# Constant matrices loaded from DRAM in place of being computed on chip, with all engine orders renewed, in a one-core SSM and gated long-convolution kernel

## The chip, the cores and the metric

The kernel runs on one core of a Trainium2 chip. The metric is device time in microseconds (us) of one execution. Five engines share the work: TensorE (PE, with its weight loads PEld), VectorE (DVE), ScalarE (ACT), GpSimd (POOL) and SyncE (SP), which here only issues DMAs.

## What is computed

Length L = 2048, 448 channels, state size N = 256. `A` is a diagonal complex SSM turned into a convolution kernel of length 2048 per channel; `B` is a gated convolution with a given kernel; a sigmoid gate mixes them.

```python
def A(u):                                  # S4 part
    K = Re sum_n C[d,n] * dt*B[d,n] * exp(dt*(A_re+1j*A_im)[d,n] * l)      # l = 0..2047 rounded to bf16
    return irfft(rfft(K, 4096) * rfft(u, 4096))[:2048] + u * Dskip
def B(q, k, v):                            # H3 part
    kv = (short convolution of k with 4 taps, shift_k) * v
    return q * (irfft(rfft(kv, 4096) * rfft(ssm_k, 4096))[:2048] + kv * ssm_D)
x = A_u;  g = sigmoid((x * gate_w).sum(-1, keepdims=True))
out = g * A(x) + (1 - g) * B(x, B_k, B_v)
```

## The kernel before, in words

The 448 channels are cut into four groups `H` of 112. A long convolution is done as a Fourier transform in stages of matmuls: `spread` (a matmul with the matrix `Wc` or `WcK`), `transform` (with `W2`, tile `s_W`), `products` on VectorE, and back with `stage_a` (matrix `R`) and `stage_b` (matrix `G`). Every stage ends in a copy out of PSUM, done by ScalarE or VectorE. `conv_B(H)` does this for part B, `conv_A(H, ..)` for part A, `table(H)` makes the SSM kernel of a group: exponentials on ScalarE (`exps`), phases and sines (`levels`), long products on VectorE (`tables`, tiles TQ and TP), a sum over states on TensorE (`sums`) and a selection of rows with one-hot matrices (`gather`). `mix` joins the halves.

Ahead of that stands a setup. `Modes.run` transposes A, B and C on TensorE with an identity, and VectorE multiplies them by dt into the tile `hold`; the four transposing DMAs of k fill `kT` (tile natu and one slot q); VectorE makes the diagonal matrices `dg` out of the taps `shift_k`; TensorE then does the short convolution of k with them (matmuls `q,natu` and `q,q`); the copies of its result are multiplied by v into natv. When the last matmul of this has read `kT`, the same tile natu takes u (`natu<-in_A_u`).

All constants are made on chip. `Consts` makes index columns with GpSimd's iota and VectorE's bit operations; `stage_c`, `stage_a` and the phases of `stage_2` and `stage_b` are turned into sines by ScalarE, `stage_2` and `stage_b` after 16 matmuls of digits with rates; `rows` and `gather` make the one-hot matrices `sel` out of 29 iotas; identity, minus identity, `one`, `sel_d` and `gx` are made by comparisons.

Nothing is left to a scheduler on the engines: `Order` collects all calls, and the string `ORDER` lists in which order they are issued, which sets the order on each engine and each queue. `SLOTS` and `ROOMS` say which of the seven SBUF slots (q0 to q6) and four PSUM rooms (ps0 to ps3) each piece takes, `SIDES` whether VectorE (V) or ScalarE (S) does a copy, a negation or a phase shift by a quarter turn (`ahead`, on ScalarE with the column `quarter`). All instructions carry the line of `issue`, L137 (L130 after the change), so tiles tell them apart, not lines. DMAs of SP and ACT use eight semaphores in turn (DMAHW0 to DMAHW7): a DMA waits until the one before it on its semaphore has landed.

Of the kernel before, what the change touches and what calls it, by code (L numbers as in the profile page):

```python
# [1014 lines left out]
```

## Time and profile before

| what | us |
|---|---|
| median of 3 runs (lowest to highest) | 261.32 (261.09 to 261.94) |
| span of the profiled execution, first to last instruction | 258.0 |
| median of the runs less that span | 3.3 |
| busy: DVE, ACT, PE, PEld, POOL | 233.3, 208.2, 205.7, 187.0, 31.0 |
| data moved by DMA | 26.44 MB, 102 GB/s on average |
| mean granted clock of TensorE | 0.963 |

The profile gives a span and no time of its own for that execution; the median of the runs stands 3.3 us above the span, and this is taken as what lies around it. Busy shares are averages over a setup (the first 50 us, in which TensorE has little to do), a long middle part in which three engines are busy nearly all the time, and an end in which the last convolution and the stores are left. The window rows below separate these.

### The profile page before, as it was taken

How to read it: one execution, taken by the hardware profiler on the slowest of the kernel's cores; microseconds unless marked ns; L12 is line 12 of the kernel's file. 1: busy time of each engine (PE TensorE's matmuls, PEld its weight loads, DVE VectorE, ACT ScalarE, POOL GpSimd, SP SyncE). 2: the span in 40 equal slices, each digit the busy share in tenths (PEclk: the TensorE clock that was granted, in tenths of full speed). 3: DMA queues.
4: the chain of work that ended last, by engine and by line, in shares of the span. 5: the costliest groups of instructions: out<-in, count | busy, mean ns of one | idle time of the engine just before them, and what ended most of it. 6: DMA issues, size and time to landing. Idle time of an engine off the chain costs nothing.

```text
span 258.0 us, 12418 instructions
## 1 busy us (share of the span) xinstructions
PE 205.7 (80%) x5631; PEld 187.0 (72%) x5631; DVE 233.3 (90%) x374; ACT 208.2 (81%) x290; POOL 31.0 (12%) x81
## 2 busy tenths in 40 slices
PE   0714679888589898989789899988999988899820
PEld 0601179887478797989778899977899967889820
DVE  6899999999788999999999999997999999958930
ACT  4829978999489999999999999999999975455300
POOL 8970002020000002100000111000121120000000
PEclk9999979999899999999999999999999999799985
DMA  6999991499872547155123327300362188000096
GB/s 147 216 195 171 171 199 24 90 176 189 148 145 37 127 127 146 35 113 131 24 64 86 74 51 167 74 5 18 78 128 39 40 176 186 5 5 3 3 176 112
DMA packets 58917, 26.44 MB, mean 102 GB/s; under 512 B 49520, under 2 KB 57200, under 8 KB 58864
## 3 DMA queue, kind: packets, MB, share of 16 engines
q1 hardware_dynamic: 52192, 18.65, 38.4%
q0 software_dynamic: 2160, 5.51, 11.9%
q10 hardware_dynamic: 4512, 1.49, 3.1%
q8 instruction: 44, 0.72, 1.2%
q14 instruction: 9, 0.07, 0.1%
HBM read 8.17 MB, written 2.52 MB: 41 GB/s over the span
## 4 chain that ended last, share of the span: by engine, by line
PE 34%; ACT 26%; DVE 17%; DMA 9%; issue 6%; SPq 3%; ACTq 0%; DVEq 0%
PE ps L137 34%; ACT q L137 22%; DVE q L137 6%; DMA natu<-in_A_u_dram 5%; DVE TP L137 5%; SPq L137 3%; DMA q<-in_A_A_re_dram 2%; DMA q<-q 2%; ACT ET L137 2%; DVE G L137 1%; ACT RK L137 1%; DVE ET L137 1%; DVE RK L137 1%; DVE natv L137 1%; ACT L137 1%
## 5 line engine op out<-in xcount | busy, mean ns | idle before, releaser
L137 ACT CAST q<-ps 128x896 bf16<-128x896 f32 (+4 forms) x165 | 137.9, 927 | 18.3 <-PE ps L137 17.0
L137 PEld LDWEIGHTS <-q 128*128 128x128 bf16 (+2 forms) x720 | 51.5, 147 | 14.1 <-issue 6.3
L137 DVE TENSOR_TENSOR TQ<-TQ,ET 128x896 bf16<-128x896 bf16 (+2 forms) x70 | 45.7, 689 | 0.1
L137 PE MATMUL ps<-q,s_W 128*128 128x112 bf16 (+1 forms) x544 | 32.8, 211 | 6.1 <-ACT q L137 5.4
L137 PE MATMUL ps<-TP,TQ 128*32 128x32 bf16 x1792 | 32.9, 240 | 3.5 <-issue 2.4
L137 PE MATMUL ps<-sa_R,q 128*128 128x128 bf16 x448 | 33.6, 229 | 1.8 <-ACT q L137 0.9
L137 PEld LDWEIGHTS <-TQ 128*32 128x32 bf16 x1792 | 30.0, 153 | 5.7 <-issue 3.5
L137 PEld LDWEIGHTS <-s_W 128*128 128x128 bf16 x544 | 27.4, 98 | 8.5 <-issue 6.8
L137 DVE TENSOR_TENSOR q<-q,q 128x3584 bf16<-128x3584 bf16 (+1 forms) x22 | 32.6, 1511 | 0.3 <-DMA q<-q 0.3
L137 POOL DMA_DIRECT2D TP<-TP x15 | 13.0, 891 | 158.7 <-DVE TP L137 41.6
L137 PEld LDWEIGHTS <-G 128*128 128x128 bf16 x1024 | 28.1, 96 | 5.1 <-issue 2.6
L137 DVE TENSOR_TENSOR TP<-TP,ET 128x1792 bf16<-128x1792 bf16 (+3 forms) x25 | 31.6, 1274 | 0.0
L137 PEld LDWEIGHTS <-natu 128*32 128x32 bf16 (+1 forms) x560 | 27.9, 181 | 4.8 <-issue 4.4
L137 PE MATMUL ps<-q,G 128*128 128x28 bf16 x1024 | 29.0, 175 | 3.0 <-issue 1.6
L137 ACT ACTIVATE q<-hold 128x224 bf16<-128x224 f32 x64 | 22.1, 407 | 0.8 <-DVE hold L137 0.8
L137 ACT ACTIVATE ET<-q 128x1344 bf16<-128x1344 int16 (+1 forms) x12 | 17.4, 1454 | 1.2 <-DVE q L137 1.1
L137 DVE TENSOR_SCALAR q<-hold 128x224 int32<-128x224 f32 x40 | 14.8, 421 | 2.8 <-ACT ET L137 2.7
L137 PE MATMUL ps<-q,q 128*32 128x336 bf16 (+3 forms) x112 | 15.0, 300 | 2.6 <-DVE q L137 2.6
L137 PE MATMUL ps<-TP 128*128 128x512 bf16 x16 | 7.8, 614 | 10.7 <-POOL TP L137 5.1
L137 PE MATMUL ps<-Wc,natv 128*64 128x128 bf16 x224 | 15.0, 284 | 1.3 <-DVE natv L137 0.9
L137 PE MATMUL ps<-q,natu 128*32 128x336 bf16 (+3 forms) x336 | 15.4, 301 | 0.5 <-DVE q L137 0.4
L137 DVE TENSOR_TENSOR TQ<-TQ 128x448 bf16<-128x448 bf16 (+2 forms) x35 | 15.6, 450 | 0.1
(82 smaller groups left out, 267.4 us busy)
## 6 DMA issues: line engine op xcount, KB each, us to landing
q<-q SPq DMA_DIRECT2D x64, 112.0 KB, 3.3
TP<-TP POOLq DMA_DIRECT2D x9, 448.0 KB, 5.1
natv<-in_B_v_dram SPq DMA_DIRECT2D x4, 448.0 KB, 7.0
...
natu<-in_A_u_dram SPq DMA_DIRECT2D x4, 448.0 KB, 10.7
...
```

Of the source, the lines that this page charges most:

```text
L137: ins = f(*args, **kw)
```

## The change

Five DRAM constants are written into the program (`inline_tensor`) and loaded by six DMAs on ACT's queue: a tile `small` takes identity and `Wc` in one DMA (128x384 bf16) and `R`, minus identity, `one`, `sel_d`, `WcK` and `sel` in another (128x1248 bf16); `W2` is one DMA (128x4096 bf16); `gx` with four mask columns is one (128x132 f32); the packed `G` is two (128x2048 bf16 each). Each half of `G` is still spread into four column groups on chip by a multiplication with a mask column (`scaled`), seven of the eight on VectorE and one on ScalarE by the new `SIDES`. All iotas, index columns, comparisons, sines and the 16 matmuls of the old constants are gone. The strings `SLOTS`, `ROOMS`, `SIDES` and `ORDER` are new from the first character to the last.

```diff
 SIDES = (
-    "SSSSSSSSSSSSSSSSSSSSSSSSSSSSSSSSSSSSSSSSSSSSSVSSSSSSSSSSSSSSSSSSVVVVVVVSS...
+    "VVSVVVVVSSSSSSSSSSSVSSSSSSSSSSSSSSSSSSSSSSSSSSSSSSSSSSSSSSSSSSSSSVSVSSSS...
 ORDER = (
-    "1 225 69 104 106 105 109 108 207 223 67-68 111 214 210-211 63 75 64 116 32 2 208 20 ...
+    "10 4 12 1 23 15 111 11 13-14 24 0 5 16 46 49-65 700 2138 706 703 709 2132 67 716 714 ...
+class Consts:
+    def __init__(self, tc, nc, pool):
+        ...
+        self.small = (
+            ("ident", 128, lambda p, c: float(p == c)),
+            ("Wc", 256, lambda p, c: turns((p % 32) * (4 * (c // 4 % 32) + 1), 128, 1 + c // 128) if c % 4 == p // 32 else 0.0),
+            ("R", 256, ...), ("minus", 128, ...), ("one", 32, ...), ("sel_d", 32, ...), ("WcK", 256, ...), ("sel", 32 * n, ...),
+        )
+        ...
+        self.tile = pool.tile([P, total], bf16, name="small")
+    def dram(self, name, cols, value, dtype=bf16):
+        return self.tc.nc.inline_tensor(np.array(table(P, cols, value), dtype=mybir.dt.np(dtype)), name="c_" + name).ap()
+    def load(self, queue, names):
+        ...
+        queue.dma_start(self.tile[:, a:b], self.dram(names[0], b - a, ...))
+    # class Sides
+    def scaled(self, dst, src, col):
+        if self.vector():
+            self.nc.vector.tensor_scalar(out=dst, in0=src, scalar1=col, scalar2=None, op0=ALU.mult)
+        else:
+            self.nc.scalar.activation(dst, src, ACT.Identity, scale=col)
     # body
-    cons = Consts(nc, wp, shaped(arena["TP"][:], [3584], i32), evac)
-    cons.rows()
+    cons = Consts(tc, nc, wp)
+    cons.load(nc.scalar, ["ident", "Wc"])
+    W2 = wp.tile([P, 32, 2, 64], bf16, name="s2_W")
+    nc.scalar.dma_start(W2[:].rearrange("p k r s -> p (k r s)"), w2)
+    cons.load(nc.scalar, ["R", "minus", "one", "sel_d", "WcK", "sel"])
+    gx = wp.tile([P, 196], f32, name="gx")
+    nc.scalar.dma_start(gx[:, 64:196], cons.dram("gx", 132, ..., f32))
+    packed = shaped(arena["TP"][:], [2, 32, 2, 32], at=10240)
+    for i in range(2):
+        nc.scalar.dma_start(packed[:, i].rearrange("p b r a -> p (b r a)"), gd[:, 2048 * i:2048 * i + 2048])
+        for g in range(4):
+            evac.scaled(G[:, 32 * i:32 * i + 32, :, g, :].rearrange("p b r a -> p (b r) a"), packed[:, i]..., gx[:, 192 + g:193 + g])
-    Wc = cons.stage_c("Wc", a1, maskg)
-    cons.turns()
-    W2 = cons.stage_2(places)
-    R = cons.stage_a(...)
-    cons.stage_b(places, G, cons.onehot(4, cons.field(0, 3)), room)
-    cons.gather(q_half, maskg)
-    WcK = cons.stage_c("WcK", aK, cons.onehot(4, cons.field(3, 3)))
```

VectorE's first rows change as follows. Before, the work on constants (TP, Wc, WcK) stands between the setup's own rows (`hold`, and the phases `q<-hold`):

```order
L137 TENSOR_TENSOR WcK<-TP 128x256
L137 TENSOR_TENSOR hold<-ps_84,TP 128x8x2x28
L137 TENSOR_SCALAR TP<-TP 128x64
L137 TENSOR_SCALAR TP<-TP 128x4
L137 TENSOR_TENSOR Wc<-TP 128x256
L137 TENSOR_SCALAR TP<-TP 128x64 x2
L137 TENSOR_SCALAR TP<-TP 128x1
L137 TENSOR_TENSOR TP<-TP 128x1
L137 TENSOR_TENSOR hold<-ps_84,TP 128x8x2x28
L137 TENSOR_SCALAR q_80<-hold 128x224
L137 TENSOR_SCALAR q_81<-hold 128x224 x2
```

Of the change, on VectorE from its first row on (`gx` holds the mask columns, RK the column dt):

```order
L906 UNCONDITIONAL_BRANCH
L130 TENSOR_SCALAR G<-TP,gx 128x64x32 x4
L130 TENSOR_TENSOR hold<-ps_84,RK 128x8x2x28 x2
L130 TENSOR_SCALAR q_80<-hold 128x224
L130 TENSOR_SCALAR q_81<-hold 128x224
L130 TENSOR_SCALAR q_80<-hold 128x224
L130 TENSOR_TENSOR q_83<-ps_84,RK 128x8x2x28
L130 TENSOR_SCALAR q_80<-hold 128x224
```

The constants' rows are gone, and half of the spreading of `G` has moved to VectorE's very start, where it waits for two loads (`G`'s first half and `gx`).

On SP's queue the loads before stand so (modes A, B, C, then the transposing DMAs of k, with gate weights between them):

```order
L137 DMA q_77<-in_A_B_re_dram 112x4x256
L137 DMA q_79<-in_A_C_re_dram 112x4x256
L137 DMA q_79<-in_A_C_im_dram 112x4x256
L137 DMA_TRANSPOSE natu<-in_B_k_dram 128x2048 [waits DMAHW0_49]
L137 DMA gw<-in_gate_w_dram 32x112 [waits DMAHW1_49]
L137 DMA_TRANSPOSE natu<-in_B_k_dram 128x2048 [waits DMAHW2_49]
```

And of the change, from the fifth DMA of SP on (DMAHW0 was last taken by the first half of `G`, issued on ACT's queue):

```order
L130 DMA q_82<-in_A_C_im_dram 112x4x256 [waits DMAHW0_49]
L130 DMA q_82<-in_A_C_re_dram 112x4x256 [waits DMAHW2_49]
L130 DMA sk<-in_B_ssm_k_dram 32x28x64 [waits DMAHW3_49]
L130 DMA sk<-in_B_ssm_k_dram 32x28x64 [waits DMAHW4_49]
L130 DMA sk<-in_B_ssm_k_dram 32x28x64 [waits DMAHW5_49]
L130 DMA dB<-in_B_ssm_D_dram 4x112 [waits DMAHW6_49,Pool_49]
L130 DMA sk<-in_B_ssm_k_dram 32x28x64 [waits DMAHW7_49]
L130 DMA_TRANSPOSE natu<-in_B_k_dram 128x2048 [waits DMAHW0_49]
L130 DMA gw<-in_gate_w_dram 32x112 [waits DMAHW2_49]
L130 DMA_TRANSPOSE natu<-in_B_k_dram 128x2048 [waits DMAHW3_49]
```

The four loads of the kernel of part B's first group (`sk`) now stand ahead of the transposes of k, and the C loads wait for semaphores that constants have taken.

On TensorE the short convolution (`natu`) came right behind the matmuls of the constants:

```order
L137 MATMUL ps_86<-TP 128x512
L137 LDWEIGHTS natu
L137 MATMUL ps_85<-q_77,natu 32x448
...
L137 LDWEIGHTS q_79
L137 MATMUL ps_85<-q_77,q_79 32x448
```

Of the change, the rows ahead of the short convolution (`sk` with `Wc`, which is now a part of `small`), and four rooms later the place where part B's first transform (`s_W`) enters it:

```order
L130 LDWEIGHTS sk
L130 MATMUL ps_86<-small,sk 64x128
L130 LDWEIGHTS natu
L130 MATMUL ps_84<-q_82,natu 32x448
...
L130 MATMUL ps_86<-q_82,q_80 32x112
L130 LDWEIGHTS s_W
L130 MATMUL ps_85<-q_77,s_W 128x112
```

All 56 `sk` matmuls of the first group moved from behind the short convolution to ahead of it, and the 64 matmuls of its transform from behind it into its middle.

More of the change, by code (lines that the diff above doesn't have):

```diff
@@ L38 @@
 SLOTS = (
-    "020260153465641042231116123354602264421130151001205634"
+    "055361130440644365524415342216505250631041526005612340"
 )
 ROOMS = (
-    "02131320012123120310303112130210300312021332031302013210231213011301130113201301221330221123000013133021310132220223"
-    "210023220032132301310012023231122032123303232020211313032101330302333110201302112031131230223"
+    "01220032103031323022130130101332312021310110300122221201131021332333023112232110023010112013232031213001012301013323"
+    "0233020031230022302231121032231303222100233131112200010233302012202323123011313023112"
 )
 SIDES = (
-    "SSSSSSSSSSSSSSSSSSSSSSSSSSSSSSSSSSSSSSSSSSSSSVSSSSSSSSSSSSSSSSSSVVVVVVVSSSSSSSSSSSSSSSSSSSSSSSSSSSSSSSSSSSSSSSSSSSVV"
-    "VVVVSSSSSSSSSSSSSSSSSSSSSSSSSSSSSSSSSSSSSVSSSSSSSSVVSSVVSSSSSSVSSSSSSSSSSSSSSSSVSSSSSSSSSVSSSSSVSSVS"
+    "VVSVVVVVSSSSSSSSSSSVSSSSSSSSSSSSSSSSSSSSSSSSSSSSSSSSSSSSSSSSSSSSSSSSSSSSSVSVSSSSSSSSSSSSSSSSSSVSSSSSSSSSSSSSSSSSSSSS"
+    "SSSSSSVVSVSVSSSSSSSSSSSSSSSSSSSSSSSSSSSSSSSSSSSSSSSSSSSSSSSVVVVVSSVSSSSSSSSSSSSSSSSSSSSVSSSSSSSSSSVSSSVSVVSS"
 )
 ORDER = (
[54 rows of a table removed]
[47 rows of a table added]
 )
@@ new lines, in table, with turns, rows, rounded @@
+def table(parts, cols, value):
+    return [[value(p, c) for c in range(cols)] for p in range(parts)]
+def turns(num, den, quarters=0):
+    return math.sin(2.0 * math.pi * ((num / den + quarters / 4.0) % 1.0))
+def rows():
+    step = [1, 2, 4, 4, 8, 8, 8, 8]
+    def rounded(grp, r, odd):
+        st = step[grp]
+        base, rem = divmod(r, st)
+        if 2 * rem > st or (2 * rem == st and (base + (odd if st == 8 else 0)) % 2):
+            base += 1
+        return base * st
+    rows, var = [], {}
+    def add(key, row):
+        var[key] = len(rows)
+        rows.append(row)
+    for r in range(8):
+        for odd in ((0, 1) if r == 4 else (0,)):
+            to = [rounded(g, r, odd) for g in range(8)]
+            add((r, odd, "own"), [Q_ROWS[256 * g + t] if t < 8 else -1 for g, t in enumerate(to)])
+            if any(t == 8 for t in to):
+                add((r, odd, "next"), [Q_ROWS[256 * g] if t == 8 else -1 for g, t in enumerate(to)])
+                add((r, odd, "last"), [Q_ROWS[256 * (g + 1)] if t == 8 else -1 for g, t in enumerate(to)])
+    return rows, var
@@ new lines, with __getitem__ @@
+class Consts:
+    def __init__(self, tc, nc, pool):
+        self.tc, self.nc, self.pool = tc, nc, pool
+        picks, self.var = rows()
+        n = len(picks)
+        q = lambda p: min(p % 32, (p % 32 + 11) >> 1)
+        self.small = (
+            ("ident", 128, lambda p, c: float(p == c)),
+            ("Wc", 256, lambda p, c: turns((p % 32) * (4 * (c // 4 % 32) + 1), 128, 1 + c // 128) if c % 4 == p // 32 else 0.0),
+            ("R", 256, lambda p, c: turns((p % 64) * (c % 64), 64, (2 * (p // 64) + 1, 2 * (p // 64), 2, 1)[c // 64]) / 2048.0),
+            ("minus", 128, lambda p, c: -float(p == c)),
+            ("one", 32, lambda p, c: float(p % 32 == c)),
+            ("sel_d", 32, lambda p, c: float(p < 4 and c == 8 * p)),
+            ("WcK", 256, lambda p, c: turns((p % 8 * 4 + p // 32) * (4 * (c // 4 % 32) + 1), 128, 1 + c // 128) if c % 4 == p // 8 % 4 else 0.0),
+            ("sel", 32 * n, lambda p, c: float(picks[c // 32][c % 8] == q(p) and c // 8 % 4 == p // 32)),
+        )
+        self.at, total = {}, 0
+        for name, m, _ in self.small:
+            self.at[name] = (total, total + m)
+            total += m
+        self.tile = pool.tile([P, total], bf16, name="small")
+    def dram(self, name, cols, value, dtype=bf16):
+        import numpy as np
+        return self.tc.nc.inline_tensor(np.array(table(P, cols, value), dtype=mybir.dt.np(dtype)), name="c_" + name).ap()
+    def load(self, queue, names):
+        a, b = self.at[names[0]][0], self.at[names[-1]][1]
+        made = [(m, f) for name, m, f in self.small if name in names]
+        cells = [(f, c) for m, f in made for c in range(m)]
+        queue.dma_start(self.tile[:, a:b], self.dram(names[0], b - a, lambda p, c: cells[c][0](p, cells[c][1])))
+    def __getitem__(self, name):
+        a, b = self.at[name]
+        return self.tile[:, a:b]
@@ L332, in col_of @@
     def col_of(self, key):
-        return self.sel[:, self.var[key]].rearrange("p a b -> p (a b)")
+        a = self.at["sel"][0] + 32 * self.var[key]
+        return self.tile[:, a:a + 32]
 class Sides:
@@ L758, in body @@
     nc.scalar.dma_start(ldt, A_log_dt.partition_broadcast(P))
-    cons = Consts(nc, wp, shaped(arena["TP"][:], [3584], i32), evac)
-    cons.rows()
+    cons = Consts(tc, nc, wp)
+    cons.load(nc.scalar, ["ident", "Wc"])
+    W2 = wp.tile([P, 32, 2, 64], bf16, name="s2_W")
+    w2 = cons.dram("W2", 4096, lambda p, c: turns(p % 64 * (4 * (32 * (c % 64) + c // 128) + 1), 8192, 1 + c // 64 % 2 - p // 64))
+    nc.scalar.dma_start(W2[:].rearrange("p k r s -> p (k r s)"), w2)
+    cons.load(nc.scalar, ["R", "minus", "one", "sel_d", "WcK", "sel"])
+    gx = wp.tile([P, 196], f32, name="gx")
+    nc.scalar.dma_start(gx[:, 64:196], cons.dram("gx", 132, lambda p, c: float(p % 32 == c % 32 if c < 128 else p % 4 == c - 128), f32))
+    packed = shaped(arena["TP"][:], [2, 32, 2, 32], at=10240)
+    gd = cons.dram("G", 4096, lambda p, c: turns((4 * (p // 4) + 1) * (64 * (c % 32) + c // 64), 8192, 1 + c // 32 % 2))
+    for i in range(2):
+        nc.scalar.dma_start(packed[:, i].rearrange("p b r a -> p (b r a)"), gd[:, 2048 * i:2048 * i + 2048])
+        for g in range(4):
+            evac.scaled(G[:, 32 * i:32 * i + 32, :, g, :].rearrange("p b r a -> p (b r) a"), packed[:, i].rearrange("p b r a -> p (b r) a"), gx[:, 192 + g:193 + g])
     modes = [qt([3, 4, 256])[0:112] for _ in range(2)]
@@ L786, in body @@
     nc.sync.dma_start(d4[:], A_Dskip.rearrange("(g l) -> g l", g=4))
-    ji = cons.carve(P)
-    nc.gpsimd.iota(ji, pattern=[[1, P]], base=0, channel_multiplier=-1)
-    ident = cons.carve(P // 2).bitcast(bf16)
-    V.tensor_scalar(out=ident, in0=ji, scalar1=0.0, scalar2=None, op0=ALU.is_equal)
-    minus = wp.tile([P, P], bf16, name="minus")
-    V.tensor_scalar(out=minus[:], in0=ident, scalar1=-1.0, scalar2=None, op0=ALU.mult)
-    dt = cons.carve(224).bitcast(bf16)
+    ident, minus, one, sel_d = cons["ident"], cons["minus"], cons["one"], cons["sel_d"][0:4]
+    Wc, R, WcK = cons["Wc"], cons["R"], cons["WcK"]
+    dt = shaped(arena["RK"][:], [448], at=448)
     nc.scalar.activation(dt, ldt, ACT.Exp)
-    a1, g1 = cons.field(0, 31), cons.field(5, 3)
-    maskg = cons.onehot(4, g1)
     dg = shaped(taps, [4, 4, 112], at=1792)
@@ L803, in body @@
                         in1=ident[:, sh:sh + 112].unsqueeze(1).unsqueeze(1).to_broadcast([P, n, 4, 112]), op=ALU.mult)
-    room = arena["TQ"][:]
-    Wc = cons.stage_c("Wc", a1, maskg)
-    cons.turns()
-    W2 = cons.stage_2(places)
-    R = cons.stage_a(cons.field(0, 63), [cons.field(6, 1, HALF, QUARTER), cons.field(6, 1, HALF, 0.0)])
-    cons.stage_b(places, G, cons.onehot(4, cons.field(0, 3)), room)
-    half = shaped(arena["TP"][:], [2, 2, 896], f32, at=3584)
+    half = shaped(arena["TP"][:], [2, 2, 896], f32, at=2688)
     held_back = qt([2, 3, M], f32)
@@ L816, in body @@
     nc.sync.dma_start(xfd[:], held_back)
-    q_col, q_half, q_cap = cons.field(0, 31), cons.carve(1).bitcast(f32), cons.carve(1)
-    V.tensor_scalar(out=q_cap, in0=q_col, scalar1=11.0, scalar2=None, op0=ALU.add)
-    V.tensor_scalar(out=q_cap, in0=q_cap, scalar1=1, scalar2=None, op0=ALU.logical_shift_right)
-    V.tensor_tensor(out=q_half, in0=q_col, in1=q_cap, op=ALU.min)
-    cons.gather(q_half, maskg)
-    aK = cons.carve(1).bitcast(f32)
-    V.scalar_tensor_tensor(out=aK, in0=cons.field(0, 7), scalar=4.0, in1=cons.field(5, 3), op0=ALU.mult, op1=ALU.add)
-    WcK = cons.stage_c("WcK", aK, cons.onehot(4, cons.field(3, 3)))
-    sel_d = wp.tile([4, 32], bf16, name="sel_d")
-    dj = cons.carve(32)[0:4]
-    nc.gpsimd.iota(dj, pattern=[[1, 32]], base=0, channel_multiplier=-8)
-    V.tensor_scalar(out=sel_d[:], in0=dj, scalar1=0.0, scalar2=None, op0=ALU.is_equal)
-    one = wp.tile([P, 32], bf16, name="one")
-    V.tensor_scalar(out=one[:], in0=cons.iota([[1, 32]]), scalar1=a1, scalar2=None, op0=ALU.is_equal)
-    gx = wp.tile([P, 192], f32, name="gx")
-    V.tensor_scalar(out=gx[:, 64:192], in0=cons.iota([[0, 4], [1, 32]]), scalar1=a1, scalar2=None, op0=ALU.is_equal)
-    assert cons.used <= 3584, cons.used
     kg = KGen(nc, places, cons, ar, arena, sel_d, d4, hold, evac)
@@ L863, in body @@
     V.tensor_tensor(out=gwt.rearrange("p n (a t) -> p n a t", t=2), in0=gw2[:].unsqueeze(2).to_broadcast([P, 112, 16, 2]),
-                    in1=one[:].rearrange("p (a t) -> p a t", t=2).unsqueeze(1).to_broadcast([P, 112, 16, 2]), op=ALU.mult)
+                    in1=one.rearrange("p (a t) -> p a t", t=2).unsqueeze(1).to_broadcast([P, 112, 16, 2]), op=ALU.mult)
     pg = places.room()[:, 0]
@@ L888, in held @@
         return consume
-    less = lambda H: (minus[:], lambda b0, n: window(ug, b0, n, H))
+    less = lambda H: (minus, lambda b0, n: window(ug, b0, n, H))
     def store(b0, n):
```

132 lines of the change are left out of this document (1 added, 131 removed), and 107 rows, old and new, of tables (ORDER, built).

## The prediction

> **What bounds the kernel now.** I read the page's span, the busy line and the chain first, then a table of stretches, then the chain in order of time.
>
> ```profile
> span 258.0 us, 12418 instructions
> PE 205.7 (80%) x5631; PEld 187.0 (72%) x5631; DVE 233.3 (90%) x374; ACT 208.2 (81%) x290; POOL 31.0 (12%) x81
> PE 34%; ACT 26%; DVE 17%; DMA 9%; issue 6%; SPq 3%; ACTq 0%; DVEq 0%
> ```
>
> VectorE is the busiest, but the chain runs mostly through TensorE and ScalarE. The stretches say why (columns: engines' busy time with instructions, granted clock, DMA share, GB/s):
>
> ```profile
> core 0: us, PE busy (x) PEld busy (x) DVE busy (x) ACT busy (x) POOL busy (x), PEclk, DMA share, GB/s
> 0.00:7.09 7.09, 0.93 (x8) 0.75 (x9) 4.08 (x31) 3.65 (x5) 5.98 (x43) 1.00 0.67 155
> 7.09:35.13 28.04, 13.33 (x86) 6.84 (x89) 27.97 (x41) 22.62 (x32) 10.45 (x21) 0.99 1.16 183
> 35.13:49.19 14.06, 13.94 (x432) 13.60 (x421) 14.06 (x23) 11.20 (x24) 1.50 (x2) 0.91 0.46 98
> 49.19:64.00 14.81, 12.66 (x224) 11.89 (x225) 14.81 (x21) 14.81 (x20) 1.75 (x2) 1.00 1.15 166
> 64.00:76.00 12.00, 8.48 (x258) 7.80 (x258) 9.76 (x15) 7.42 (x13) 0.00 (x0) 0.86 0.75 147
> 76.00:200.00 124.00, 113.84 (x3321) 106.91 (x3321) 120.07 (x182) 121.97 (x166) 8.42 (x10) 1.00 0.39 81
> 200.00:242.60 42.60, 38.61 (x1189) 35.61 (x1188) 38.07 (x60) 26.56 (x35) 2.87 (x4) 0.96 0.29 63
> 242.60:258.00 15.40, 3.93 (x131) 3.55 (x130) 4.49 (x9) 0.00 (x1) 0.00 (x0) 0.72 0.70 121
> ```
>
> From 7.09 to 35.13 VectorE alone is full (27.97 of 28.04 us) and DMA is at its limit (share 1.16); TensorE has half its time free. From 76 to 200 all three are full, ScalarE most (121.97 of 124). At the end TensorE leads. Between, one hole: 64 to 76, where ScalarE is free for 4.6 us, TensorE for 3.5, VectorE for 2.2. The chain names its cause, the load of u:
>
> ```profile
> 0.74 5.27 DMA q<-in_A_A_re_dram
> ...
> 45.59 3.57 PE ps L137 x90
> ...
> 53.58 14.14 DMA natu<-in_A_u_dram
> ```
>
> The short convolution ends at 49.2 and frees natu, u lands at 67.7, and TensorE waits for it. The first row is where the chain begins, the load of A_re.
>
> **The change, part by part.** First VectorE's setup, in order of time:
>
> ```profile
> 7.09 0.62 DVE L137 TENSOR_TENSOR hold<-ps,TP 128x448 f32<-128x448 bf16 x1 [1.57 <-PE ps L137]
> 7.63 1.89 DVE L137 TENSOR_SCALAR TP<-TP 128x64 int32<-128x64 int32 x2
> 7.98 1.54 DVE L137 TENSOR_TENSOR Wc<-TP 128x256 bf16<-128x256 bf16 x1
> 8.31 1.32 DVE L137 TENSOR_SCALAR TP<-TP 128x64 int32<-128x64 int32 x3
> 9.53 4.74 POOL L137 IOTA TP<- 128x2 int32 x7
> 10.40 7.53 DVE L137 TENSOR_SCALAR q<-hold 128x224 int32<-128x224 f32 x8
> 19.48 0.71 DVE L137 TENSOR_TENSOR ga_sel<-TP 128x544 bf16<-128x544 f32 x1
> 29.30 1.55 DVE L137 TENSOR_TENSOR q<-q,TP 128x1344 bf16<-128x1344 bf16 x1
> 35.13 0.62 DVE L137 TENSOR_TENSOR TQ<-hold,ET 128x896 bf16<-128x896 bf16 x1
> ```
>
> *Constants on VectorE.* What runs before 7.09 (4.08 us) hides behind the first load; taking it out gains nothing. Behind 7.09 stand 2.1 us (7.63 to 9.74) and 0.9 us (`ga_sel` and a mask): 3.0 us on the path.
>
> *GpSimd's iotas.* The eight phases at 10.40 take 7.5 us. The same instruction later in the kernel, and GpSimd's like, read:
>
> ```profile
> L137 DVE TENSOR_SCALAR q<-hold 128x224 int32<-128x224 f32 x30 | 6.8, 274 | 2.8 <-ACT ET L137 2.7
> L137 POOL IOTA TP<- 128x2 int32 x19 | 2.1, 130 | 0.1
> L137 DVE TENSOR_SCALAR G<-TQ,TP 128x2048 bf16<-128x2048 bf16 x8 | 5.9, 752 | 0.0
> L137 ACT ACTIVATE s_W<-ps 128x1024 bf16<-128x1024 int16 x4 | 3.9, 1042 | 0.0
> L137 ACT ACTIVATE TQ<-ps 128x1024 bf16<-128x1024 int16 x4 | 3.8, 1016 | 0.0
> L137 ACT ACT_TABLE_LOAD x9 | 11.5, 1283 | 1.3 <-PEq L999 1.2
> L137 PE MATMUL ps<-TP 128*128 128x512 bf16 x16 | 7.8, 614 | 10.7 <-POOL TP L137 5.1 <-DVE TP L137 2.6 <-ACT TQ L137 1.6
> L137 PE MATMUL ps<-Wc,sk 128*64 128x128 bf16 x224 | 8.1, 221 | 0.4 <-DVE sk L137 0.3
> L137 PE MATMUL ps<-q,s_W 128*128 128x112 bf16 x480 | 30.8, 214 | 6.1 <-ACT q L137 5.4 <-issue 0.6
> L137 DVE TENSOR_TENSOR TQ<-TQ,ET 128x896 bf16<-128x896 bf16 (+2 forms) x70 | 45.7, 689 | 0.1
> ```
>
> Thirty phases cost 6.8 us, 0.23 each, so eight should take 1.8: 5.7 us are lost while GpSimd works, and GpSimd's own small iotas stretch beside them (seven in 4.74 us). With GpSimd empty there I count 5.6 us as gained; the bounds are 0 (the slowness is something else) and 5.7. The Trainium skill, "SBUF — State Buffer", section "Who interferes with whom", says that GpSimd and a VectorE instruction in a two-port mode lock each other out of a shared port for whole instructions; by it all 5.7 us go, without it the sum below has 5.6 less. The trace agrees in the stretching of both engines (940 against 227 ns, 677 against 130 ns).
>
> *VectorE until the table.* From the first `hold` to the first long product (35.13) it needed 28.0 us; after: 28.0 - 3.0 - 5.6 = 19.4. Of the eight spreads of `G` (0.74 us each) three lay in this stretch and five behind; now four stand ahead of `hold`, three in the stretch, one on ScalarE (2048 columns, some 2 us by twice a sine of 1024).
>
> *Start.* Before, `hold` waits for A_re only. Now it waits for identity too, and behind the four spreads for `G`'s half and `gx`, while 0.67 of the DMA time was already in use. The bytes wanted first (0.52 MB of `G`, 0.28 MB of small ones, 0.46 of A) need 6.9 to 8.1 us at the 183 to 155 GB/s of the first two stretches; A_re alone took 5.3. I take 8.0 for `G`, 2.7 for four spreads (0.74 each, issued a little closer): `hold` at 10.7, 3.6 us later. Bounds: 0 (the loads hide as A_re does, the spreads before it) and 6 (identity behind all of these). VectorE reaches the long product at 30.1 rather than 35.1.
>
> *Transposes of k.* They gate the short convolution once VectorE is faster:
>
> ```profile
> 5.36 4.78 SPq L137 DMA_TRANSPOSE natu<-in_B_k_dram  x1
> 17.34 2.71 SPq L137 DMA_TRANSPOSE natu<-in_B_k_dram  x1
> natu<-in_B_k_dram SPq DMA_TRANSPOSE x3, 5.8
> ```
>
> Before, the first left at 5.36, the last at 17.34, landing at about 23. TensorE met them at 31 to 34, because the tap matrices (29.30) were late:
>
> ```profile
> 31.00 0.43 PE L137 MATMUL ps<-q,natu 128*32 128x448 bf16 x3 [0.44 <-DVE q L137]
> 34.07 0.35 PE L137 MATMUL ps<-q,q 128*32 128x448 bf16 x1 [2.64 <-DVE q L137]
> 17.74 0.86 ACT L137 ACTIVATE q<-q,quarter 128x672 int32<-128x672 int32 x1 [4.71 <-POOL natu L137]
> ```
>
> The last row is ScalarE's, for below. After, C_im waits for `G`'s half (8.0) and takes as long as A_re, 5.3 us, and only then the first transpose leaves: 13.3, 8 us later. The last would land at 31; beside it the `sk` loads (0.46 MB), the rest of `G` (0.5 MB) and `W2` (1 MB) pass the same DMA engines. Ends: 31 and 41 (1.5 MB at 158 GB/s per full share, 183 / 1.16, all ahead). I take 33.5, near the lower end since `W2` leaves ScalarE's queue behind its first sine, at 23 or later. The tap matrices are ready at about 28 (29.30 + 1.55, less the 5.0 of above, and the smaller second part), so k is what the convolution waits for: 33.5 against 34.07 before. The cover of 8 to 10 us that k had is used up.
>
> *TensorE.* The 16 matmuls (7.8 us) lay in its free time: no gain. The convolution took 15.1 us (34.07 to 49.19); the 64 transform matmuls now inside it cost 64/480 x 30.8 = 4.1 us, so it ends at 52.7, with 4.1 us of transforms and 56/224 x 8.1 = 2.0 us of `sk` already done: 2.6 us ahead. Then u takes its 18.5 us again (49.19 to 67.7): 71.2. In the new order 768 matmuls (sums, spreads, transforms) stand between; at the rate of 76 to 200 (113.84 us for 3321) these are 26 us, so the 3.5 us hole closes: 6.1 us in all.
>
> *ScalarE.* Later start +3.6; the wait for slowed phases at 17.74 gone, -4.7; eight sines -7.7; of two table loads fewer, one on the path, -1.3; spread of `G` +2.0; five quarter-turn shifts that the new `SIDES` moves over from VectorE, three of 672 columns at 0.86 and two of 896 at 1.15, +4.9 (copies and negations move both ways and about cancel); hole of 64 to 76 closed, -4.6. Sum: -7.8.
>
> *VectorE overall.* +3.6 - 8.6 - 3.7 (five spreads not left for later) - 3.5 (five shifts of 672 or more columns, 0.7 each as three times a phase of 224): -12.2. It isn't the one that binds any more.
>
> *Sum.* Copies by ScalarE and matmuls by TensorE alternate in the middle, so the path gains what the slower of them gains: between 6.1 and 7.8, taken as 7.3, nearer to ScalarE, which is the fuller one from 76 to 200. The span falls to 250.7; with 3.3 around it, 254.0. From 76 us on I expect no change of rate.
>
> **Rivals.**
> (1) *VectorE was the bound throughout.* For it: 90% busy. Then its 12.2 us count whole: 261.3 - 12.2 = 249.1, and if copies can move back onto it, its hole of 2.2 closes and ends nearer 244. Against: ScalarE's 121.97 of 124.
> (2) *The middle eats the gain.* ScalarE is given 4.9 us more work where it is full, and u still comes as late as now (49.19 before, 52.7 after, plus 14.14 of landing). If the hole stays and the start costs 6, the gain is 0 to 2: 259 to 261.3.
> (3) *The constants' loads are the new bound: slower.* The place is the transposes of k behind C_im, `G` and `sk`. If they land at 41 or later, TensorE, ScalarE's copies and the load of u all move: each us past 33.5 costs one, so from 7.3 us late, at 40.8, the kernel loses. At 44, 264.5. For it: DMA share 1.16 in just that stretch. The Trainium skill, "DMA: Bandwidth & Descriptors", section "Issuing engines are not separate DMA queues", speaks for it: queues of different engines share 16 DMA engines and interleave, so ACT's queue gives constants no road of their own. Its 358 GB/s for HBM would make the 2.6 MB an estimated 7 us, where the rows' 158 GB/s make 16. The share of 1.16 agrees that they would collide.
> (4) *The change doesn't do what it says:* a GpSimd memset of k's padding (slot q3) now stands behind an accumulating DMA that waits for VectorE's 22nd long product: 30.1 + 22 x 0.69 = 45.3. TensorE gets there after five of eight rooms and the transforms, 33.5 + 5/8 x 15.1 + 4.1 = 47.0. If VectorE is 4 us late, TensorE waits 2: 256. Small, and inside my range.
>
> **How the numbers follow.** Forecast (250 to 257.5, from the bounds of the start and of the transposes near their taken values): 0.60. Rival 1: 0.16. Rival 2: 0.12, half of it within 0.3% of the time before (0.8 us, about what a measurement of this kernel tells from no change). Rival 3: 0.10, of it 0.02 a loss under 0.3%. Rival 4 sits in the forecast; the remaining 0.02 is for the new order as such, to either side. Faster: 0.60 + 0.16 + 0.06 + 0.01 = 0.83; same: 0.06 + 0.02 = 0.08; slower: 0.08 + 0.01 = 0.09. Below 246 I leave out half of rival 1 (0.08), above 261.5 the 0.11 of losses. The bounds of the unknown terms (start 0 to 6, lock 0 to 5.7, k at 31 to 41) lie within that.
>
> **What the profile after would show.** GpSimd idle in the first 10 us and the ten early phases at 0.23 to 0.28 us each (wrong if near 0.9). `hold` at 9 to 12 us. TensorE's first `natu` matmul at 31 to 36 us, waiting for a DMA and not for VectorE; later than 40 makes the prediction wrong. No wait for u on TensorE. VectorE's busy time near 216 us (233.3 - 4.1 - 3.0 - 5.6 - 0.7 - 3.5), ScalarE's near 204, with VectorE below ScalarE in most stretches after 76; if VectorE is full there and ScalarE not, rival 1 holds.

## The result, and the profile after

Slower: 281.98 us (median of 4, 280.13 to 283.72) against 261.2 beside it, ratio 1.081 with a 95% interval of 1.073 to 1.089. The forecast was 254.0. What lies around the span is 1.8 us (the profiled execution took 280.13), not the 3.3 that the forecast added. Some executions of each kernel take 1 to 4% longer than its others; medians are of all, ratios of the others alone, so costs in us are taken from the ratios, as parts of 260 us. The page of the changed kernel, in the lines that answer to the first ones above:

```profile
span 278.3 us, 12286 instructions
PE 206.7 (74%) x5615; PEld 191.0 (69%) x5615; DVE 220.9 (79%) x328; ACT 206.0 (74%) x283; POOL 14.9 (5%) x28
PE 31%; ACT 25%; DVE 18%; issue 9%; DMA 8%; SPq 5%; ACTq 0%; DVEq 0%
```

The work went down, though by less than reckoned: VectorE by 12.4 us (17 forecast), ScalarE by 2.2 (4). The span is 20.3 us longer all the same, so all three engines stand idle more. The stretches (same columns as before the change, cut where something ends) show where:

```profile
0.00:10.71 10.71, 1.65 (x16) 1.51 (x16) 2.74 (x4) 1.86 (x2) 1.09 (x10) 1.00 0.86 197
10.71:35.07 24.36, 6.75 (x89) 6.04 (x89) 18.21 (x31) 18.75 (x29) 0.00 (x0) 1.00 1.11 197
35.07:48.45 13.38, 6.04 (x112) 5.12 (x112) 11.07 (x19) 4.81 (x11) 0.00 (x0) 0.82 1.21 161
48.45:63.67 15.22, 14.79 (x370) 13.85 (x371) 11.36 (x19) 15.19 (x23) 2.05 (x3) 0.82 0.74 178
63.67:84.00 20.33, 15.17 (x403) 14.27 (x404) 20.12 (x26) 18.41 (x21) 0.86 (x1) 0.92 1.01 155
84.00:96.00 12.00, 10.60 (x337) 9.83 (x337) 5.53 (x10) 8.10 (x11) 0.00 (x0) 0.72 0.02 4
96.00:130.00 34.00, 30.85 (x780) 28.83 (x777) 33.24 (x39) 32.62 (x53) 2.58 (x3) 1.00 0.57 113
130.00:150.00 20.00, 16.93 (x602) 15.81 (x601) 14.42 (x26) 14.75 (x18) 0.00 (x0) 0.83 0.33 76
150.00:190.00 40.00, 35.30 (x908) 32.60 (x909) 39.23 (x49) 39.47 (x49) 2.58 (x3) 1.00 0.29 60
190.00:210.00 20.00, 18.04 (x516) 16.84 (x507) 15.03 (x35) 15.48 (x26) 0.80 (x2) 0.91 0.22 50
```

Two faults lie ahead of 63.67, the end of the short convolution (before: 49.1): TensorE has 6.75 of 24.36 us until it starts, and from 35.07 to 48.45 ScalarE has 4.81 of 13.38. The third lies behind: three stretches (from 84, 130 and 190 us) in which VectorE and ScalarE stand idle for 4 to 6.5 us each. The timeline of TensorE and ScalarE names the first two (in brackets: idle time before the row, and what ended it):

```profile
35.07 0.59 PE L130 MATMUL ps<-q,natu 128*32 128x448 bf16 x3 [12.39 <-ACT q L130]
```

```profile
23.38 0.67 ACT L130 ACTIVATE q<-hold 128x224 bf16<-128x224 f32 x2 [4.83 <-DVE hold L130]
...
25.00 1.28 ACT L130 ACT_TABLE_LOAD   x1
...
32.21 1.28 ACT L130 ACT_TABLE_LOAD   x1
...
34.45 1.48 ACT L130 CAST q<-ps 128x512 bf16<-128x512 f32 x2
...
37.85 0.96 ACT L130 ACTIVATE q<-hold 128x224 bf16<-128x224 f32 x3
47.02 0.33 ACTq L130 DMA_DIRECT2D small<-c_R  x1
47.39 1.01 ACT L130 CAST q<-ps 128x1024 bf16<-128x1024 f32 x1 [8.57 <-DMA natv<-in_B_v_dram]
```

(1) In the new order TensorE spreads `sk` ahead of the convolution, into the PSUM rooms. The copies that free the rooms stand in ScalarE's row behind a wait of 4.83 us for VectorE's `hold`, two table loads and three sines, so TensorE's wait of 12.39 us ends with a copy. But k is no earlier by much: its last packets end at 34.1 us in the DMA records (21.6 before), for its transposes stand behind `sk` and later C loads now. (2) The load of R's block is a DMA in ScalarE's own row. It waits for a semaphore that the fourth load of v used last, v lands at 47, and ScalarE with all copies of the convolution stands still for 8.57 us.

### The profile page after: what moved, and what is told of

Read it like the earlier page. It is cut to its first block, busy times and chain, and to the rows that moved or that the text cites. A ratio compares the mean times of both kernels' runs of the same rounds, so it can differ in the third digit from the quotient of the medians.

```text
span 278.3 us, 12286 instructions
## 1 busy us (share of the span) xinstructions
PE 206.7 (74%) x5615; PEld 191.0 (69%) x5615; DVE 220.9 (79%) x328; ACT 206.0 (74%) x283; POOL 14.9 (5%) x28
## 4 chain that ended last, share of the span: by engine, by line
PE 31%; ACT 25%; DVE 18%; issue 9%; DMA 8%; SPq 5%; ACTq 0%; DVEq 0%
PE ps L130 31%; ACT q L130 20%; DVE TP L130 6%; SPq L130 5%; DVE TQ L130 4%; DVE q L130 4%; DMA natv<-in_B_v_dram 3%; ACT ET L130 3%; DMA q<-in_A_B_im_dram 3%; DVE natu L130 1%; ACT RK L130 1%; DMA sk<-in_B_ssm_k_dram 1%; DVE RK L130 1%; DVE ET L130 1%; DMA q<-q 1%
## 5 line engine op out<-in xcount | busy, mean ns | idle before, releaser
L130 ACT CAST q<-ps 128x1024 bf16<-128x1024 f32 (+3 forms) x165 | 139.6, 925 | 26.5 <-PE ps L130 17.5
L130 PE MATMUL ps<-small,q 128*128 128x128 bf16 (+1 forms) x496 | 37.9, 237 | 12.4 <-DMA small<-c_ident 8.5
L130 PE MATMUL ps<-q,s_W 128*128 128x112 bf16 (+1 forms) x544 | 36.0, 219 | 13.8 <-ACT q L130 8.4
L130 PEld LDWEIGHTS <-s_W 128*128 128x128 bf16 x544 | 29.9, 102 | 16.3 <-issue 14.2
L130 PEld LDWEIGHTS <-natu 128*32 128x32 bf16 (+1 forms) x560 | 29.9, 184 | 15.3 <-issue 13.6
L130 PEld LDWEIGHTS <-TQ 128*32 128x32 bf16 x1792 | 29.9, 153 | 10.5 <-issue 9.8
L130 DVE TENSOR_TENSOR TP<-TP,ET 128x1792 bf16<-128x1792 bf16 (+3 forms) x25 | 31.6, 1275 | 0.4
L130 PE MATMUL ps<-q,natu 128*32 128x336 bf16 (+3 forms) x336 | 17.7, 324 | 12.7 <-ACT q L130 12.7
L130 ACT CAST RK<-ps 128x448 bf16<-128x448 f32 (+1 forms) x16 | 11.6, 723 | 13.2 <-PE ps L130 13.1
L130 PE MATMUL ps<-small,natv 128*64 128x128 bf16 x224 | 15.6, 303 | 3.0 <-DVE natv L130 2.2
L130 PE MATMUL ps<-q,q 128*32 128x336 bf16 (+3 forms) x112 | 17.2, 323 | 0.0
L130 PEld LDWEIGHTS <-natv 128*64 128x64 bf16 x224 | 14.8, 213 | 3.6 <-DVE natv L130 2.4
```

The lines of the kernel that those rows point to most:

```text
L130: ins = f(*args, **kw)
```

## The experiments

What bears on the verdicts, by kernel: the ratio to the kernel before, and from the profiled execution the first and the last matmul of the short convolution (TensorE's timeline) and the rest of the span behind it.

| kernel | constants, order | ratio to before (95%) | conv from, to | rest |
|---|---|---|---|---|
| before | made, old | 1 | 31.0, 49.1 | 208.9 |
| traffic | made, old, loads for nothing on ScalarE's queue | 1.070 (1.061 to 1.080) | 40.1, 64.8 | 209.3 |
| traffic_sync | the same on SyncE's queue | 1.012 (1.007 to 1.016) | 31.4, 52.4 | 209.8 |
| old_order | loaded, old | 1.058 (1.048 to 1.068) | 33.9, 62.2 | 210.0 |
| old_order_sync | the same, SyncE's queue | 1.017 (1.012 to 1.023) | 25.8, 53.8 | 210.3 |
| old_late | loaded behind `xfd` (SyncE's store of a tile q to DRAM, 37.5 us), old | 1.000 (0.995 to 1.004) | 23.1, 40.8 | 216.2 |
| free_old | neither made nor loaded, old | 0.990 (0.984 to 0.995) | 23.8, 42.4 | 209.9 |
| free_new | neither, new | 1.047 (1.042 to 1.053) | 31.6, 55.8 | 213.9 |
| r_on_sync | after, R's load on SyncE | 1.064 (1.056 to 1.071) | 35.1, 59.3 | 217.0 |
| after_sync | after, loads on SyncE | 1.083 (1.077 to 1.090) | 40.8, 65.0 | 216.1 |
| after | loaded, new | 1.081 (1.073 to 1.089) | 35.1, 63.7 | 214.6 |

The theories: 1, R's blocked load is the loss; 2, the loads hinder k and the rest of the start; 3, the new order loses in itself.

**R's load off ScalarE's late queue.** `r_on_sync`: `cons.load(nc.sync, ["R", ...])` at the same place of `ORDER`. `r_early`: call 3 moved in `ORDER` behind call 5.

> The changed kernel with one DMA issued by another engine: the load of R, minus, one, sel_d, WcK and sel stands in SyncE's queue behind the natv loads, no longer in ScalarE's. Theory 1 (this DMA holds ScalarE's queue for 8.6 us, from 38.8 to 47 us, and the conv and all behind it with that): ScalarE's wait of 8.6 us goes, the conv ends near 55 us in place of 63.7, and the total comes down from 282.0 by 7 to 10 us, to 272 to 275. Theory 2 (the loads at the start delay identity, transposes and k): nothing changes before 35 us, so the total stays within 2 us of 282. Theory 3 (the new order is slower from 60 us on, whatever the conv does): the conv ends earlier, but the total comes down by 3 us at most.

> The changed kernel with that same load moved to the head of ScalarE's queue, behind the second G load and ahead of ScalarE's first computation. Theory 1: as with SyncE, 272 to 275 us. Theory 2: the load's 312 KB are now in the way of the first transposes and the k transposes, so the start gets later by 1 to 2 us, and the total is 1 to 2 us above that of the run with the load on SyncE. Theory 3: 279 us or more.

277.23 us (275.84 to 280.53) and 277.13 (275.45 to 280.65), by the ratios (1.064 and 1.063) 4.5 and 4.7 us of the 21. ScalarE's wait for v is gone, the convolution ends 4.4 us earlier. Theory 1 is true, but it had 7 to 10 us, and explains about a fifth of the loss. This run also shows how close k is behind the copies: here the convolution starts at 35.09, and its fourth matmul waits for k's last landing.

```profile
35.93 0.59 PE L130 MATMUL ps<-q,q 128*32 128x448 bf16 x1 [0.25 <-DMA q<-in_B_k_dram]
```

**The start in another order.** `start_first`: identity first, A's loads next, four spreads of G behind A's scaling.

> The changed kernel with the start in another order: identity and Wc first, then log_dt and Exp, A's two loads, gx, the G halves and R's block; the first four spreads of G on VectorE stand behind the scaling of A. R's block is so off ScalarE's later queue as well. Theory 1: 272 to 275, the same as with R's block early. Theory 2: hold's start comes earlier by 2 to 3 us, the total is 2 to 3 us under that of the run with R's block early, 269 to 272. Theory 3: 278 or more.

280.14 us (ratio 1.074), no gain on `r_early`: the convolution starts at 37.2. VectorE now waits for G's half between its phases, so `hold` is 2.1 us later than in the changed kernel, ScalarE waits 8.4 us for it ahead of the same sines and copies, and k's last packets end at 37.1. None of the theories said that.

**The old order with loaded constants.** `old_order`: the strings of the kernel before, with constants' calls struck out and the loads at the head of ScalarE's queue.

```diff
 ORDER = (
-    "10 4 12 1 23 15 111 11 13-14 24 0 5 16 46 49-65 ...
+    "1 0 15-20 46 4-5 10 3 2 111 34 49-56 65 701 ...
```

> The loaded constants with the order, slots, rooms and sides of the kernel before: the instructions that made constants are gone, the eight spreads of G stand where they stood, on VectorE, and the six loads of constants stand at the head of ScalarE's queue (identity and Wc, log_dt, Exp, then gx, both G halves, R's block, W2); G's packed copy lies in TQ rows 0 to 9 in place of TP. Theory 3 (the search of a new order did the harm): it is at or under the kernel before, 252 to 261 us, for some 10 us of work of ScalarE and VectorE ahead of 50 us are gone. Theory 2 (the loads themselves delay the start): 262 us or more, with the conv's end behind 49.1 us. Theory 1 alone (one blocked load in the new order): 252 to 258, for no load stands behind a natv load here.

277.38 us, ratio 1.058: in the old order the loads cost 15 us (12.4 to 17.7). Theory 3 fell as the only cause, theory 1 too, since no load is blocked here.

**The loads without the change.** `traffic`: the kernel before with six loads of the same sizes into G and W2, which are overwritten later. `traffic_sync`: the same with one word changed, and in `ORDER` the load of identity's size moved behind those of A, B and C.

```diff
-        nc.scalar.dma_start(dst, c)
+        nc.sync.dma_start(dst, c)
```

> The kernel before, with all its constants still made on chip in its own order, and six added loads of the same sizes as the changed kernel's (2.58 MB of zeros, at the head of ScalarE's queue, into G and W2, which are overwritten later by the made constants). Theory 2, as it now stands after the run with the old order (the loads take the DMA engines while k's DMA transposes are to run, the conv waits for k): the k transposes end near 37 us in place of 20, the conv ends 12 to 15 us later than 49.1, and the total is 270 to 280 us. Theory 3 (the new order did the harm) and theory 1 (one load blocks ScalarE's queue): nothing of this in the kernel before, 259 to 263 us.

> The run traffic again (the kernel before with 2.58 MB of added loads that nothing uses), with the six loads on SyncE's queue, behind A, B and C's loads and ahead of k's DMA transposes, in place of ScalarE's queue. Theory 2a (the bytes ahead of k are the cost): 2.58 MB at the 260 GB/s of the profile's second slice are 10 us, and k's transposes then run alone as in the kernel before: 268 to 272 us. Theory 2b (what costs is that two queues' packets alternate on the DMA engines, so that k's 256 B packets go at a fifth of their pace): with one queue no alternating, so also about 10 us here, but 18 us in the run traffic, 7 to 9 us apart. If the two runs are within 2 us, at 276 to 280, the queue does not matter and each byte costs more than its transfer.

277.8 us and 263.5: 18 us on ScalarE's queue, 3 on SyncE's, where k's transposes stand too. SyncE's timeline, the first, second and last transpose of k, in `traffic` and then in `traffic_sync` (start, duration of the issue; before: 4.78 for the first, 2.71 for the last):

```profile
8.06 14.07 SPq L137 DMA_TRANSPOSE natu<-in_B_k_dram  x1
...
23.32 14.76 SPq L137 DMA_TRANSPOSE natu<-in_B_k_dram  x1
...
40.97 2.84 SPq L137 DMA_TRANSPOSE natu<-in_B_k_dram  x1
```

```profile
11.91 7.00 SPq L137 DMA_TRANSPOSE natu<-in_B_k_dram  x1
...
19.59 4.89 SPq L137 DMA_TRANSPOSE natu<-in_B_k_dram  x1
...
27.48 2.12 SPq L137 DMA_TRANSPOSE natu<-in_B_k_dram  x1
```

Beside the loads of the other queue the issue of each of the first two transposes takes 14 to 15 us, behind them on its own queue 5 to 7. And these two rows of the page of `traffic` (slices of 6.9 us) show that it isn't for bytes: the DMA engines are busy in nine tenths or more from the second slice to the ninth while only 66 to 138 GB/s pass from the fourth to the sixth, where 261 passed in the second:

```profile
DMA  6999999998998624734632332730144259200086
GB/s 154 261 135 85 66 138 185 168 173 190 171 183 154 107 52 105 161 63 89 137 54 54 89 69 48 166 61 6 38 94 80 37 119 194 67 5 2 2 153 119
```

In the trace's DMA records k's 8192 packets of 256 B take 13.6 us in the kernel before, 33.6 in `traffic` and 16.0 in `traffic_sync`. I had 10 us for the bytes in either theory. The 3 found are fewer, for in the kernel before the tap matrices hold the convolution until 31.0 whatever k does up to then; in `traffic_sync` it starts at 31.4 and takes 20.9 us in place of 18.1, at a mean granted clock of 0.79 in place of 0.91.

In `traffic` the taps are late as well: their load stands behind the constants on ScalarE's queue, and takes from 16.04 to 38.32.

```profile
38.35 1.56 DVE L137 TENSOR_TENSOR q<-q,TP 128x1344 bf16<-128x1344 bf16 x1 [8.18 <-DMA q<-in_B_shift_k_dram]
45.88 0.60 PE L137 MATMUL ps<-q,natu 128*32 128x448 bf16 x2 [5.23 <-DMA natu<-in_B_k_dram]
```

The second row is TensorE's: k's last landing is the later one, so k and not the taps decides here. What slows both queues when they run side by side, no run shows.

`old_order_sync` asks the same with loaded constants (gx, G, R and W2 moved to `nc.sync`):

> The run old_order again (loaded constants, order of the kernel before, 277.4 us), with gx, both G halves, R's block and W2 on SyncE's queue behind A, B and C's loads and ahead of k's DMA transposes; identity and Wc and log_dt stay on ScalarE's. Theory 2b (two queues alternating on the DMA engines slow k's transposes): the transposes' packets take 14 to 16 us in place of 27.6, the conv ends near 50 us in place of 62.2, and the total is 258 to 264. Theory 2a (bytes alone): the same bytes stand ahead of k, 273 or more.

264.75 against 277.38 us, ratios 1.017 and 1.058: the queue is 10.5 us of the 15. The convolution starts at 25.8, 5 us earlier than before, but ends at 53.8, not 50: TensorE waits 4.8 us for k's later landings, and VectorE, which multiplies the copies by v, waits for v, whose loads stand behind k:

```profile
46.26 1.16 DVE L133 TENSOR_TENSOR natv<-q,natv 128x896 bf16<-128x896 bf16 x2 [8.52 <-DMA natv<-in_B_v_dram]
```

In `old_order` the same wait is 8.5 us, in `traffic` 5.5: loads that delay k delay v with it. `old_gfirst` then left only gx and G ahead of k:

> The run old_order_sync again (264.8 us), with only gx and the two G halves (1.1 MB) ahead of k on SyncE's queue, and W2 and R's block behind xfd, ahead of u; the spreads of G stand where they stood in the kernel before. Theory 2a/2b (one queue: the cost is the bytes ahead of k, 1.4 MB less than in old_order_sync at 260 GB/s): 5 us less before the conv, 257 to 261. If VectorE's start and not the conv is the bound: 262 to 266.

267.49 us, ratio 1.025: wrong. The convolution starts at 25.7 and ends at 54.0 as in `old_order_sync`, k's packets took 19.1 us though no second queue was in the way, and u lands at 73.0 in place of 72.6. Why k was slower with fewer bytes ahead, and where the other 2 us went, stays open.

**Loads out of k's way.** `old_late`: old order, identity and Wc first, the other loads on SyncE behind xfd, G's packed halves in free parts of G and RK, the spreads later.

> The loaded constants in the order of the kernel before, as in the run with the old order, but only identity and Wc (96 KB) ahead of k; W2, G, gx and R's block stand on SyncE's queue behind natv, sk and xfd, G's packed halves lie in G itself and in RK, and the eight spreads of G stand on VectorE ahead of the first use of RK. Theory 2: the k transposes end near 20 us again, the conv ends at or before 49 us, and with the constants' work gone the total is 250 to 259 us. If instead the loaded constants cost time wherever they stand (u and sk late behind 2.5 MB, W2 late): 262 to 272.

258.73 us, the same as the kernel before. The convolution ends 8.3 us earlier, and the loads take it back one step on, where u stands behind them:

```profile
42.07 18.16 SPq L133 DMA_DIRECT2D natu<-in_A_u_dram  x4
```

```profile
66.43 1.86 PE L133 MATMUL ps<-natu,q 128*32 128x64 bf16 x56 [9.63 <-DMA natu<-in_A_u_dram]
```

Four attempts to keep that gain moved the loads about: W2 ahead of `sk` and G behind u (`old_split`), G whole without spreads (`old_full`), W2 and R ahead of u (`old_mix`), G behind `sk`'s second loads too (`old_mix2`).

> The run old_late again (loaded constants, order of the kernel before, identity and Wc first), with W2 behind natv, R's block and gx behind xfd, the u loads next and G's packed pieces behind u; G's spreads on VectorE behind table 0's last product (four of 2048, four of 1536, four of 512 columns, one 512-column piece in a tile of its own). Theory 2 (what stands ahead of a needed load on the DMA engines decides): TensorE's wait of 9.6 us for u goes, the conv still ends near 41 us, and the total is 249 to 253 us. If the time after the conv is bound by VectorE's tables whatever u does: 256 to 260.

> The run old_split with G loaded whole, 4 MB in ten pieces (seven behind u, three behind the first swaps), in place of 1 MB and twelve spreads: 6 us of VectorE's work go, 3 MB of traffic come. If VectorE's work bounds the middle: 3 to 6 us under old_split. If the loads delay the swaps of the transformed tables, which share SyncE's queue: 3 to 8 us above it.

> The run old_split again, with W2 and R's block behind xfd, then u, then gx and G's pieces (in old_split W2 stood ahead of sk, and the conv ended at 46.9 in place of 40.8). Theory 2: the conv ends near 41 us as in old_late, u comes by 53 us and TensorE's wait for u is gone: 248 to 255. If VectorE bounds the rest, whose idle time in its first 10 us (waiting for hold) is 7.3 us in place of 3.0 with constants made on chip: 256 to 261, as in old_late.

> The run old_mix again with gx and G's pieces behind sk's second loads as well (in old_mix VectorE waited 7.0 us for those, behind G). If that wait and not the work is what old_mix had over old_late: 3 to 7 us under old_mix, 258 to 262. If the late loads' other delays go too (conv end near 41, rest 209 as with the old order elsewhere): 250 to 256. If late loads disturb the conv in any order (ends at 46): 262 or more.

265.43, 267.6, 267.46 and 267.31 us (ratios 1.010, 1.028, 1.017, 1.018), all worse than `old_late` (1.000), the first of them barely. In `old_mix` VectorE waits 7.0 us for `sk`'s second half. TensorE's granted clock is recorded at 0.50 when the convolution starts there, but 49 matmuls run from 26 to 28 us as against 48 in `old_late`. With `sk` ahead (`old_mix2`) nothing came back. What remains of these is only that 2.5 MB found no free place in the first 70 us; which of the delays decides was not settled.

**The new order without the loads in its way.** `new_late`, `new_late2`: late loads in the new order, W2 behind and ahead of v. `after_sync`: all but identity and log_dt on SyncE.

> The changed kernel's own order, slots, rooms and sides with the same late loads behind natv on SyncE's queue and the same late spreads (seven on VectorE, one on ScalarE). Theory 2: the start is freed, the conv ends near 50 us, and the total is 252 to 262 us, close to that of the old order with late loads. Theory 3: 5 us or more above the run with the old order and late loads, for the mid-stalls from 84 us on stay.

> The run new_late again (the changed kernel's own order with late loads), with W2's load ahead of natv, for in this order TensorE uses W2 inside the conv and waited 10 us for it. Theory 2: without that wait 270 to 276 us. Theory 3 (the new order is worse in itself): it stays 10 us or more above the run old_late (258.7), for sk's loads stand ahead of k's transposes in SyncE's order and the middle's stalls stay.

> The changed kernel with the same done to it: its own order, gx and both G halves behind A's loads on SyncE's queue, W2 and R's block behind B and C's loads, ahead of sk and k; identity and Wc and log_dt alone on ScalarE's queue. So neither R's wait on ScalarE nor the alternating of two queues is left. Theory 2b alone (the loads' queue was all of the loss): 258 to 265, the same as old_order_sync. With theory 3 beside it (the new order loses in itself, by sk ahead of k and by the stalls from 84 us on): 270 to 277.

285.32, 280.73 and 282.42 us (ratios 1.097, 1.077, 1.083): whatever was done for the loads, the new order stayed at 280 or above. In `after_sync` this tells less than I meant it to, since `sk`, k and G came later there and the convolution started at 40.8. So the last two runs left the loads out: GpSimd sets G and W2 to one number in the first 10 us.

```diff
-    nc.sync.dma_start(W2[:]..., w2)
+    nc.gpsimd.memset(W2[:]....bitcast(f32), 0.0078...)
```

> What the constants cost at most: the order, slots, rooms and sides of the kernel before, with G (32 KB in each partition) and W2 neither made nor loaded, but set to one number by GpSimd in the first 12 us, so that the computed values are not the reference's; identity and Wc are loaded first, R's block and gx (0.38 MB) behind xfd. If the making of the constants stood on the path in the kernel before: 246 to 252. If it was covered (VectorE waits for hold anyway while it makes constants; old_late, at no gain): 255 to 260. Against old_late (258.7) the difference is what the 2.1 MB of late loads and the spreads cost there.

> The same in the changed kernel's order, slots, rooms and sides: G and W2 set to one number by GpSimd in the first 15 us, R's block and gx behind natv on SyncE's queue, no other load of constants but identity and Wc. If the loads were all of the loss: the same as free_old within 2 us. Theory 3 (the new order loses in itself): 8 to 20 us above free_old, with the part behind the conv's end 214 to 218 us long in place of 209 to 211.

256.61 and 272.32 us. This splits the loss in three steps, as parts of 260 us from the ratios: constants for nothing, old order, -2.7; the new order on top, +15.0; the loads and G's spreads on top, +8.8, of which R's blocked load is 4.5. The split hangs on its sequence: with the loads first they cost 17.7 (`old_order` over `free_old`), and the new order on top 6.0, for both hold up the same start (33.9 with the loads, 31.6 with the new order, 35.1 with both). In `free_new` TensorE's wait ahead of the convolution is there without the constants' loads (waits: total, times, longest), and so are the stretches with sums:

```profile
PE ps L130 <- ACT q L130: 19.9, 12, 12.3
```

```profile
130.00:140.00 10.00, 8.72 (x288) 8.09 (x287) 5.23 (x11) 5.74 (x8) 0.00 (x0) 0.74 0.58 117
140.00:180.00 40.00, 36.24 (x876) 33.61 (x874) 38.81 (x51) 39.18 (x46) 2.58 (x3) 1.00 0.29 60
180.00:190.00 10.00, 7.55 (x323) 6.90 (x320) 5.86 (x13) 5.54 (x13) 0.00 (x0) 0.83 0.10 24
```

By its profile 13.4 us of the order's loss lie ahead of the convolution's end (55.8 against 42.4 in `free_old`) and 4.0 behind. Of the 13.4, 7.8 lie ahead of its start, and three things come late there at once: ScalarE's copies, k (first transpose at 11.87 against 4.16, behind `sk`; last packets end at 29.8 against 21.9) and the tap matrices (28.7 against 23.6 for their first part). The copies come last, but k alone would hold the start to within 2 us of where it is; no run took them apart. The other 5.6 lie inside the convolution, where the transforms now stand. Behind it, TensorE's row holds runs of 256, 192 and 384 matmuls of `sums` without another between, 5.7, 4.9 and 8.7 us long, where the old order has 192 and 160; VectorE and ScalarE have nothing to copy meanwhile. That the runs cause the 4.0 us is read from the idle time beside them; no run split them.

## Why the prediction was wrong, step by step

Two steps failed: TensorE's, by which the convolution ends at 52.7 (63.67 measured), and the one that put the new order as such at next to nothing (15.0 us without loads, 6.0 on top of them). The gain that was to stand against them was too large as well.

- *VectorE's setup and GpSimd's iotas: right up to the phases, wrong behind them.* `hold` was forecast at 10.7 and starts at 10.71; the ten early phases at 0.23 to 0.28 us each, and three take 0.65 together. The four spreads end 0.9 us earlier, `hold` then waits for dt:

```profile
7.11 2.74 DVE L130 TENSOR_SCALAR G<-TP,gx 128x2048 bf16<-128x2048 bf16 x4 [7.11 <-DMA gx<-c_gx]
10.71 1.16 DVE L130 TENSOR_TENSOR hold<-ps,RK 128x448 f32<-128x448 bf16 x2 [0.86 <-ACT RK L130]
11.90 0.65 DVE L130 TENSOR_SCALAR q<-hold 128x224 int32<-128x224 f32 x3
```

  The first long product was forecast at 30.1 and came at 37.76: VectorE waits 3.49 and 3.88 us for ScalarE's row on the way, which the sum of VectorE's own work did not hold.
- *Transposes of k: nearly right, with a condition missing.* The first was to leave at 13.3 and left at 15.19; the convolution was to start at 33.5 and started at 35.07. k was as late as forecast (last packets end at 34.1), but the wait that ended last was for ScalarE. The step took the convolution's two inputs, k and taps, as its only conditions and did not follow the copies that free its PSUM rooms through ScalarE's row. Here that cost a us or less; in `start_first` and `after_sync`, which moved loads, the copies came later still (37.2, 40.8).
- *TensorE: failed.* The convolution was to take 15.1 us and 4.1 of transforms, to 52.7; it ended at 63.67. Of these 28.6 us, 4.4 are R's blocked load (`r_on_sync`: 24.2). Of the 5.0 that `r_on_sync` still has over the 19.2, 4.3 are three more waits for ScalarE's copies. The term had no line for a DMA that waits in a computing engine's row, though the order listed both.
- *"From 76 us on I expect no change of rate": failed.* By TensorE's step the part behind the convolution was to get shorter by 9.6 us (6.1 of work done earlier, 3.5 of the hole); it got longer by 5.7, and by 4.0 between `free_old` and `free_new`. The 2 in 100 for the new order as such was the worst number of all.
- *No wait for u: right*, and of no use, since TensorE is late by then. *Busy times*: VectorE 220.9 for 216, ScalarE 206.0 for 204.
- *The sum.* Even without the new faults the 7.3 us were too much: `free_old` gains 2.7 (1.4 to 4.1) with all constants for nothing. There the first long product starts at 25.93 in place of 35.13, so VectorE's term was real; but VectorE then waits 4.65 us for v, and 6.7 of the 9.2 us are left at the convolution's end. Its profiled execution, the shortest (254.48 us), is 5.7 us under the one before; in the ratio 2.7 arrive. What takes the rest is open.
- *Rival 3* had a mechanism that is real, transposes of k beside the constants' loads, but its condition (k at 41 or later) did not come about in the changed kernel. In the old order it is the loss: k's last landing moves from 22.9 to 39.4 us, and the loss is 15, near its price of a us for each us. The Trainium skill, "DMA: Bandwidth & Descriptors", section "Issuing engines are not separate DMA queues", says that such queues interleave on the same engines; the runs agree, and 277.8 against 263.5 us for the same bytes is more than sharing explains: on one queue k's last packets end at 31.5 us, behind all the loads, on two at 45.4.

No version beat the kernel before in full; `old_late` equals it.
